# Moving the lane swaps of a spatial product on TensorE: cuts at 10, 19 and 38 of 48 instead of 12, 20 and 32

## The chip, the cores and the metric

One core of one Trainium2 chip. The metric is the device time of one execution in microseconds (us); of several runs the median is taken.

## The reference

```python
xn = _layernorm(x)                                   # x: 1 x 2048 x 512
# A: attention, 32 heads of 16
qkv = xn @ wqkv
p = softmax(q @ k.T * 16 ** -0.5); o = p @ v
A = o @ wo
# B: gated MLP with a product over the positions
z = gelu(xn @ w_in)                                  # 2048 x 1792
z1, z2 = z[..., :896], _layernorm(z[..., 896:])
g = einsum("ts,bsf->btf", w_sp, z2) + b_sp[:, None]  # w_sp: 2048 x 2048
B = (z1 * g) @ w_out
out = x + A + B
```

The step that this case is about is g, the *spatial* product: every output column block (128 of the 896 features) is a sum over all 2048 positions.

## The kernel before, in words

Everything is written out as one stream per engine by a planner that runs while the program is built. After a start of some 130 us the work goes in **rounds**. A round (the loop over `b` from L1521) holds four steps of attention: 8 score matmuls (`st`, in `score`, L1274, each followed by an exponential on ACT, `pf`, L1277), 8 matmuls for the row maxima of later scores (`mx`, in `max_one`, L904, each followed by a reduction on DVE, L905), then a share of **dense** matmuls of the other branches (one line, `lane`, L233), and at the end 16 matmuls that multiply the probabilities with v (`o`, in `pv`, L1232). So each round shows as one block of 16 `o` matmuls, and the time from one block's start to the next is the time of a round. Row maxima run 26 steps ahead of the scores. There are 256 such blocks; we number the rounds as `b` does (b = 286, 290, ...).

TensorE is used as two **lanes**: rows 0 to 63 of the array and rows 64 to 127, side by side. Scores and maxima take one lane each. A dense product has 128 rows, so it is cut into a half for each lane, and the two halves of one accumulator must not write its PSUM bank at the same time. A group of two blocks therefore has two accumulators (banks `d0`, `d1`), and `halves` (L252) gives each lane another one: a **pair** is one matmul on lane 0 for one accumulator and one on lane 1 for the other. Each accumulator has 48 products (16 tiles of 128 positions, 3 products for each tile, since numbers are split into a high and a low part), so a group has 96 pairs. `cuts` says after how many products the lanes change accumulators. With cuts (12, 20, 32) the first accumulator's products 0 to 11 go on lane 0 while the second's 0 to 11 go on lane 1; then they swap, and each lane does products 0 to 19 of the other; then 12 to 31, then 20 to 47, then 32 to 47: **runs** of 12, 20, 20, 28 and 16 pairs.

```python
for k, stop in enumerate([*cuts, total, total]):
    turn_ = k % 2
    while at[turn_] < stop:
        i, j = divmod(at[turn_], 3)
        ...
        yield END if last else SWAP if at[turn_] == stop else 1
```

A swap ends what `gather` may collect: a round holds pairs of one run only. `share` then divides the collected run evenly over rounds: a run of r pairs takes at most r // 8 rounds, and at most about 13 pairs go in one. That gives the numbers of dense pairs in a round. When a tile that a product needs isn't there by the planner's clock, the run is collected up to that product and the rest waits (`yield -2`). `fill` orders the matmuls of a round by a randomised search over its own cost model.

`spatial` (L717) has 16 groups: for each of four stripes of w_sp, three groups of two blocks and one single block of 48 pairs. For two-block groups the cuts depend on `want`, the pairs that the planner would like to place in a round: (12, 24, 36) above 11.4, (12, 20, 36) above 10.2, and the third choice below. We number the groups 0 to 15. The third choice is taken by groups 0, 1, 2, 4, 5, 6, 8, 9, 10 and 14. The z2 tiles of a group (`zs`, four quarters for each block, 512 KB each) are loaded on SP by `load_z`: a quarter is asked for in `done(s)` when both accumulators have passed tile 3, 7, 11 or 15; the first of these asks for the fourth quarter of the own group, and the planner counts it as there 0.8 + 4.0 us later at the earliest. After a group, DVE adds a row to the first accumulator (L807) and ACT copies the second (L78); both free the banks for the next group.

Of the kernel before, what the change touches and what calls it, by code (L numbers as in the profile page):

```python
# [55 lines left out]
def fused_block(ctx, tc, x, wqkv, wo, w_in, w_spT, b_sp, w_out, out):  # L56
# [19 lines left out]
    def act(out, in_, func, n, ago=1.2, **kw):  # L76
        load["A"] = max(load["A"], clock() - ago) + 0.18 + n / 1200.0
        return nc.scalar.activation(out, in_, func, **kw)  # L78

    def dve(n, rate=1):  # L80
        load["D"] = max(load["D"], clock() - 1.2) + 0.065 + n / (960.0 * rate)
        return nc.vector
# [38 lines left out]
    def move(dst, src):  # L121
        dma[0] = max(dma[0], clock()) + 0.1 + 4e-6 * math.prod(dst.shape) / FLOW
        nc.sync.dma_start(raw(dst), raw(src))
# [7 lines left out]
    def slow(us, fn, *args):  # L131
        later(us, waiting.append, (fn, args))
# [10 lines left out]
    def clock():  # L143
        return max(lanes)

    def gps(us):
        pool[0] = max(pool[0], clock()) + us
        return nc.gpsimd
# [24 lines left out]
    def later(us, fn, *args):  # L173
        late.append((clock() + us, len(late), fn, args))
# [20 lines left out]
    def piece(nm):  # L195
        return big.tile([P, 2, 512], F32R, tag="big", name=nm, bufs=RING)

    def t512(nm):
        return big.tile([P, 512], F32, tag="t512", name=nm, bufs=4)

    def hilo(nm):
        return big.tile([P, 2, 512], F32R, tag="hilo", name=nm, bufs=3)
# [22 lines left out]
    def three(lhs, rhs):  # L225


        (lh, ll), (rh, rl) = lhs, rhs
        return [(lh, rh), (ll, rh), (lh, rl)]
# [46 lines left out]
    def whole(accs, cells, done=None):  # L276


        for i in range(len(cells)):
            while True:  # L280
                prods = cells[i]()
                if prods is not None:
                    break
                yield -2
            for j in range(3):
                last = i == len(cells) - 1 and j == 2
                for half in range(2):
                    lane(accs[half], half, prods[j], i == 0 and j == 0, last)
                if j < 2:
                    yield 1  # L290
            if done:
                posts.append(partial(done, i))
            yield END if last else 1
# [8 lines left out]
    def dpair(nm):  # L302
        return [dpsum(f"{nm}_{u}", f"d{u}") for u in range(2)]
# [27 lines left out]
    def prepare(out, loads, freed=None):  # L331


        loads, flight, made = list(loads), [], []
        while loads or flight or made:
            if made and clock() >= made[0][0]:
                _, k, t = made.pop(0)
                out[k] = t
            if flight and clock() >= flight[0][0]:
                _, k, l = flight.pop(0)  # L340
                t = end(l)
                made.append((pool[0], k, t))
                rawfree.append(pool[0])
            if loads and len(rawfree) > 0 and clock() >= rawfree[0] and (freed is None or freed and clock() >= freed[0]) and (not steady or dma[0] <= clock() + BACK):
                rawfree.pop(0)
                if freed:
                    freed.pop(0)
                k, *a = loads.pop(0)
                l = begin(*a)
                flight.append((dma[0] + LAND, k, l))  # L350
            yield

    def prime():

        next(queue[1])
# [291 lines left out]
    def wait(k, gen):  # L647
        yield from until(clock() + k)
        yield from gen

    def z1_gelu(f, g, x, u):
        gelu_in(x, u, 512)
        yield from pool_done(LAG)
        yield from calm()
        act(u, u, AF.Tanh, 512, scale=GC)
        yield from ready("A")
        gelu_out(x, u, 512, 0.5)
        gelued.append((f, g))
        yield
# [53 lines left out]
    def sp_weights(g, s):  # L713
        return f"wsp{g}_{s}", w_spT[s * P:(s + 1) * P, g * 512:(g + 1) * 512], 512


    def spatial():  # L717
        zp, z1s, hls = {}, {}, {}

        def load_z(g, f, i):  # L720
            t = piece(f"zs{g}_{f}_{i}")
            move(t.rearrange("p a (s f) -> p a s f", f=P), z2scr[:, f, :, 4 * i:4 * i + 4, :])
            later(4.0, zp.update, {(g, f, i): t})

        def load_z1(g, f):
            z1s[g, f] = x = t512(f"z1i{g}_{f}")
            move(x, z1scr[f][:, g, :])
            hls[g, f] = hilo(f"hhl{g}_{f}")
            side.append(wait(10.0, z1_gelu(f, g, x, hls[g, f][:, 0, :].bitcast(F32))))

        def load_b(g):
            move(brow, b_sp[4 * g:4 * g + 4, :].rearrange("(o a) b -> o (a b)", o=1).to_broadcast([P, 512]))

        groups = [(g, [f, f + 1] if f + 1 < NF else [f]) for g in range(NG) for f in range(0, NF, 2)]
        ahead = [(g, f, i) for g, fs in groups for i in range(4) for f in fs]
        while len(stored) < NT:
            yield -1
        load_b(0)
        for _ in range(4):
            load_z(*ahead.pop(0))  # L740
        yield -4
        for _ in range(2):
            load_z(*ahead.pop(0))
        for n, (g, fs) in enumerate(groups):
            accs = dpair(f"sp{g}_{fs[0]}")
            last_, single = n == len(groups) - 1, len(fs) == 1
            if single and g + 1 < NG:
                freed = [clock()] * 2
                bg.append(prepare(wsp, [((g + 1, s), *sp_weights(g + 1, s)) for s in range(NT)], freed))

            def prods(f, s):
                zt, sl = zp[g, f, s // 4], slice((s % 4) * P, (s % 4 + 1) * P)
                w = wsp[g, s]
                return three((zt[:, 0, sl], zt[:, 1, sl]), (w[:, 0, :], w[:, 1, :]))

            def part(s):
                if (g, s) not in wsp or any((g, f, s // 4) not in zp for f in fs):
                    return None
                return prods(fs[0], s) if single else [prods(f, s) for f in fs]

            def done(s):
                if s == 7:
                    for f in fs:
                        load_z1(g, f)
                if single and g + 1 < NG:
                    freed.append(clock() + 1.0)
                if last_:
                    nonlocal_freed(s)
                if s % 4 == 3:
                    for _ in fs:  # L770
                        if ahead:
                            slow(0.8, load_z, *ahead.pop(0))

            tail = []

            def nonlocal_freed(s):
                if s == 0:
                    bg.append(prepare(wout, [(f, f"wout{f}", w_out[f * P:(f + 1) * P, :], 512) for f in range(NF)], tail))
                if s < NF:
                    tail.append(clock() + 1.0)  # L780
                if s == NT - 5:
                    prime()

            cells = [(lambda s=s: part(s)) for s in range(NT)]
            want = STEPS * pace + credit / 4
            cuts = (12, 24, 36) if want > 11.4 else (12, 20, 36) if want > 10.2 else (12, 20, 32)
            if single:
                yield from whole(accs, cells, done)
                f = fs[0]
                hl = hls[g, f]  # L790
                t = hl[:, 1, :].bitcast(F32)
                act(t, accs[0], AF.Copy, 512)
                dve(512).tensor_add(t, accs[1], t)
                gps(1.3).tensor_add(t, t, brow)
                side.append(h_split(g, f, z1s[g, f], hl))
                if g + 1 < NG:
                    later(done_by("P"), load_b, g + 1)
            else:
                yield from halves(accs, cells, cuts, done)
                for u, f in enumerate(fs):  # L800
                    hl = hls[g, f]
                    t = hl[:, 1, :].bitcast(F32)
                    if u:
                        act(t, accs[u], AF.Copy, 512)
                        gps(1.3).tensor_add(t, t, brow)  # L805
                    else:
                        dve(512).tensor_add(t, accs[u], brow)  # L807
                    side.append(h_split(g, f, z1s[g, f], hl))
            yield 0
# [815 lines left out]
```

## Time and profile before

| | us |
|---|---|
| median of 3 runs (1789.13 to 1792.41) | 1790.3 |
| the profiled execution | 1790.37 |
| its span, first to last instruction | 1788.3 |
| TensorE busy in it | 1777.3 (99%) |
| DVE busy | 1449.6 (81%) |
| ACT busy | 1267.0 (71%) |
| GpSimd (POOL) busy | 782.5 (44%) |

TensorE is busy nearly all the time, at a granted clock of 0.999, but a busy TensorE is not a TensorE at its peak: matmuls overlap, and their ends are modelled. What a round costs is read from the starts of the `o` blocks.

### The profile page before, as it was taken

To read this page: it belongs to the slowest core of one execution; us is meant where nothing else is said; L and a number is where in the kernel's file an instruction comes from. 1 tells how busy PE (TensorE), PEld (TensorE's weight loads), DVE (VectorE), ACT (ScalarE), POOL (GpSimd) and SP (SyncE) were. 2 spreads that over 40 slices of the span, in tenths; PEclk is the share of its full clock that TensorE was granted. 3 is DMA by queue.
4 is the path that set the end of the run, shared out by engine and by line. 5 is a ranking of instruction groups with operands and counts; after the bars stand their busy time and mean duration, and the time that the engine had idled before them with its cause. 6 is when DMAs were issued, how large, how long until landed. Compare 5 with 4: busy or idle time off the path is not lost.

```text
span 1788.3 us, 37962 instructions
## 1 busy us (share of the span) xinstructions
PE 1777.3 (99%) x14419; PEld 1140.7 (64%) x14419; DVE 1449.6 (81%) x2604; ACT 1267.0 (71%) x2351; POOL 782.5 (44%) x815
## 2 busy tenths in 40 slices
PE   9999999999999999999999999999999999999998
PEld 7876666666666666666666566666666666666664
DVE  5288888988888888888888888888877888888872
ACT  5338788887777777777777777777776777677765
POOL 4257676777412542257334573224765261003220
PEclk9999999999999999999999999999999999999999
DMA  7552443534645744356445564345766454454534
GB/s 282 201 171 78 133 127 104 170 88 125 198 150 172 221 140 116 109 171 183 133 144 176 173 195 115 105 126 164 200 180 179 142 169 134 149 170 150 160 108 135
DMA packets 218254, 274.63 MB, mean 154 GB/s; under 512 B 35752, under 2 KB 119352, under 8 KB 216632
## 3 DMA queue, kind: packets, MB, share of 16 engines
q1 hardware_dynamic: 215336, 263.47, 49.1%
q0 software_dynamic: 2592, 8.46, 1.2%
q8 instruction: 114, 1.87, 0.5%
q14 instruction: 68, 0.56, 0.1%
q10 hardware_dynamic: 144, 0.26, 0.0%
HBM read 178.55 MB, written 93.58 MB: 152 GB/s over the span
## 4 chain that ended last, share of the span: by engine, by line
PE 96%; DMA 1%; DVE 1%; ACT 1%; SPq 0%; issue 0%; POOL 0%; DVEq 0%; POOLq 0%; ACTq 0%
PE o L1232 26%; PE st L1274 18%; PE sp L233 17%; PE mx L904 13%; PE z2p L233 5%; PE mo L233 4%; PE z1p L233 3%; PE qk L233 3%; PE ao L233 2%; PE duo L233 2%; PE v L221 1%; PE v L222 1%; PE v L223 1%; DMA zs<-z2scr 0%; PE qk L221 0%; PE qk L222 0%
## 5 line engine op out<-in xcount | busy, mean ns | idle before, releaser
L905 DVE TENSOR_REDUCE mm<-mx 128x1 f32<-128x512 f32 x2048 | 1291.2, 685 | 249.4 <-PE mx L904 214.6
L1277 ACT ACTIVATE pf<-st 128x512 f32<-128x512 f32 x2048 | 1102.9, 601 | 361.9 <-PE mx L904 211.1
L1274 PE MATMUL st<-qst,kst 50*128 50x512 f32 x2048 | 764.4, 410 | 0.8 <-ACT pf L1277 0.7
L904 PE MATMUL mx<-kst,qst 48*128 48x512 f32 x2048 | 752.3, 412 | 0.1
L1274 PEld LDWEIGHTS st<-qst,kst 50*128 50x128 f32 x2048 | 361.0, 185 | 248.1 <-issue 116.8
L233 PE MATMUL sp<-wsp,zs 64*128 64x512 f32 x2688 | 510.2, 393 | 0.0
L1232 PE MATMUL o<-pf,vall 128*32 128x512 f32 x4096 | 492.5, 598 | 0.0
L904 PEld LDWEIGHTS mx<-kst,qst 48*128 48x128 f32 x2048 | 361.8, 185 | 63.4 <-ACT pf L1277 11.6
L233 PEld LDWEIGHTS sp<-wsp,zs 64*128 64x128 f32 x2688 | 366.2, 186 | 29.9
L1232 PEld LDWEIGHTS o<-pf,vall 128*32 128x32 f32 x4096 | 107.0, 109 | 235.2 <-issue 215.7
L233 PE MATMUL mo<-wout,hp 64*128 64x512 f32 x672 | 124.5, 392 | 0.0
L233 PEld LDWEIGHTS mo<-wout,hp 64*128 64x128 f32 x672 | 90.5, 186 | 9.6
L539 POOL TENSOR_TENSOR hhl<-z1i 128x512 f32<-128x512 f32 x28 | 29.2, 1042 | 148.0 <-DMA z1i<-z1scr 118.4
L78 ACT ACTIVATE e<-o 128x512 f32<-128x512 f32 x64 | 38.4, 599 | 70.0 <-PE o L1232 65.8
L861 POOL TENSOR_TENSOR xr<-mox,xr 128x512 f32<-128x512 f32 x8 | 10.3, 1285 | 131.3 <-ACT mox L78 131.3
L545 POOL TENSOR_SCALAR hhl<-hhl 128x512 f32<-128x512 f32 x28 | 17.4, 621 | 104.0 <-ACT hhl L78 104.0
L967 POOL TENSOR_TENSOR ob<-ob 128x512 f32<-128x512 f32 (+1 forms) x16 | 20.7, 1292 | 96.3 <-DMA ob<-rscr 96.3
L805 POOL TENSOR_TENSOR hhl<-hhl,brow 128x512 f32<-128x512 f32 x12 | 15.4, 1287 | 83.5 <-ACT hhl L78 80.7
L233 PE MATMUL ao<-wo,op 64*128 64x512 f32 x288 | 51.9, 392 | 0.0
L586 POOL TENSOR_TENSOR z<-z,z2u 128x896 fp32r<-128x896 f32 x16 | 34.1, 2130 | 27.4 <-ACT z2u L78 27.4
L1039 POOL TENSOR_TENSOR fin<-aox,fin 128x512 f32<-128x512 f32 x8 | 10.3, 1282 | 74.9 <-ACT aox L78 74.9
L233 PEld LDWEIGHTS ao<-wo,op 64*128 64x128 f32 x288 | 36.4, 186 | 4.1
(293 smaller groups left out, 1955.6 us busy)
## 6 DMA issues: line engine op xcount, KB each, us to landing
zs<-z2scr SPq DMA_DIRECT2D x112, 512.0 KB
escr<-e SPq DMA_DIRECT2D x60, 256.0 KB
hscr<-hhl SPq DMA_DIRECT2D x28, 512.0 KB
xscr<-xnT POOLq DMA_DIRECT2D x16, 512.0 KB, 4.9
qscr<-qkhl SPq DMA_DIRECT2D x16, 512.0 KB
kscr<-qkhl SPq DMA_DIRECT2D x16, 512.0 KB
qst<-qscr SPq DMA_DIRECT2D x128, 64.0 KB
hp<-hscr SPq DMA_DIRECT2D x16, 512.0 KB
```

The source lines that it names most:

```text
L78: return nc.scalar.activation(out, in_, func, **kw)
L221: nc.tensor.matmul(acc, lh, rh, start=first, stop=False)
L222: nc.tensor.matmul(acc, ll, rh, start=False, stop=False)
L233: made[half] = lambda: nc.tensor.matmul(acc, prod[0][rows], prod[1][rows], start=start, stop=stop)
L539: gps(0.0022 * n).tensor_mul(u, x, x)
L586: gps(2.1).tensor_sub(low, z, u)
L904: nc.tensor.matmul(acc, qst[c][rows, t * P:(t + 1) * P], kst[p % 2][rows, kc * 512:(kc + 1) * 512], start=True, stop=True)
L905: nc.vector.tensor_reduce(mmax[i // 16][:, j, t, kc:kc + 1], acc, AX.X, ALU.max)
L967: gps(1.3).tensor_mul(both[rows, 0, :], both[rows, 0, :], both[rows, 2, :])
L1232: nc.tensor.matmul(acc[cols:cols + VW, a:a + w], vpack(kt - 1 + r, 2 * p + j), pf[:, j * 512 + a:j * 512 + a + w], start=kt == 1 and a == ...
L1274: nc.tensor.matmul(st, kst[p % 2][rows, kt * P:(kt + 1) * P], qst[c][rows, :], start=True, stop=True)
L1277: nc.scalar.activation(full[n][:, j * 512:(j + 1) * 512], st, AF.Exp, scale=0.25)
```

## The change

The third choice of `cuts` becomes (10, 19, 38): runs of 10, 19, 28, 29 and 10 pairs, 96 as before, with four swaps as before.

```diff
-            cuts = (12, 24, 36) if want > 11.4 else (12, 20, 36) if want > 10.2 else (12, 20, 32)
+            cuts = (12, 24, 36) if want > 11.4 else (12, 20, 36) if want > 10.2 else (10, 19, 38)
```

Counted in the order of the built programs, the dense pairs in the rounds of a group are:

| groups | before | changed |
|---|---|---|
| 1, 2, 4, 5, 6, 8, 9 | 12, 10 10, 10 10, 10 9 9, 8 8 | 10, 10 9, 9 9 10, 10 10 9, 10 |
| 0 | the same | 10, 10 9, 12 14 2, 10 10 9, 10 |
| 10 | the same | 10, 10 9, 13 13 2, 10 10 9, 10 |
| 12 to 14 (27 rounds, b = 710 to 814) | 12 times 12; 11 11 13 13; five 10; three 9; two 8; one 3 | 19 times 12; 15 11 10; three 9; 6; 3 |
| the rounds after that | the same numbers | the same, one round earlier |
| last round of all (b = 1022) | 12 | 0 |

Before, the cuts of group 12 and 13 were (12, 24, 36) and group 14 had the third choice; in the changed program all three have (12, 24, 36), since by its counts `want` is higher when they begin. Groups 0 to 11 begin at the same steps in both programs.

Three places show what moves on TensorE (PE). The names: `st` is a score, `mx` a row maximum, `sp` a spatial product with its accumulator's number, `wsp` and `zs` its operands, `o` the product with v. First, the beginning of the round b = 470, the first of group 5, before:

```order
L1274 MATMUL st_0_12953<-qst_86,kst_90 128x512
L904 MATMUL mx_1_12961<-kst_90,qst_88 128x512
L1274 MATMUL st_0_12964<-qst_86,kst_90 128x512
L1274 MATMUL st_1_12973<-qst_86,kst_90 128x512
L904 MATMUL mx_0_12976<-kst_90,qst_88 128x512
L233 MATMUL sp_2_1_12952<-wsp_0_11512,zs_3_0_12593 128x512
L233 MATMUL sp_2_0_12951<-wsp_0_11512,zs_2_0_12574 128x512
```

and in the changed program:

```order
L1274 MATMUL st_1_12951<-qst_86,kst_90 128x512
L904 MATMUL mx_0_12961<-kst_90,qst_88 128x512
L233 MATMUL sp_2_1_12950<-wsp_0_11523,zs_3_0_12667 128x512
L233 MATMUL sp_2_0_12949<-wsp_0_11523,zs_2_0_12657 128x512
L904 MATMUL mx_1_12966<-kst_90,qst_88 128x512
L1274 MATMUL st_0_12969<-qst_86,kst_90 128x512
```

The first dense matmul stood sixth and now stands third, ahead of three matmuls of attention. Second, the round b = 674 of group 10 in the changed program, whole but for its `o` block (before, the same round has 20 dense matmuls):

```order
L1274 MATMUL st_0_17603<-qst_87,kst_89 128x512
L904 MATMUL mx_1_17607<-kst_89,qst_88 128x512
L233 MATMUL sp_4_1_17151<-wsp_12_15491,zs_5_3_17480 128x512
...
L233 MATMUL sp_4_0_17150<-wsp_12_15491,zs_4_3_17465 128x512
L1274 MATMUL st_1_17644<-qst_87,kst_89 128x512
L233 MATMUL sp_4_1_17151<-wsp_12_15491,zs_5_3_17480 128x512
L233 MATMUL sp_4_0_17150<-wsp_12_15491,zs_4_3_17465 128x512
L904 MATMUL mx_0_17649<-kst_89,qst_88 128x512
```

These four dense matmuls (two pairs) are all that was left of the run: the two that read the fourth quarter `zs_4_3`, `zs_5_3`. Third, the end of the last round, b = 1022, in the changed program:

```order
L1274 MATMUL st_1_25859<-qst_88,kst_90 128x512
L1274 MATMUL st_0_25863<-qst_88,kst_90 128x512
L1274 MATMUL st_1_25866<-qst_88,kst_90 128x512
L1274 MATMUL st_0_25870<-qst_88,kst_90 128x512
L1232 MATMUL o_3_25694<-pf_25811,vall 32x512 x2
L1232 MATMUL o_3_25694<-pf_25818,vall 32x512 x2
L1232 MATMUL o_3_25694<-pf_25861,vall 32x512 x2
L1232 MATMUL o_3_25694<-pf_25868,vall 32x512 x2
```

Before, 24 dense matmuls stand between the third of these scores and the fourth; they have moved to earlier rounds.

## Rows read from the trace of the kernel before

**Rows 1.** The page: span, busy time of each engine, costliest DVE group.

```profile
span 1788.3 us, 37962 instructions
...
PE 1777.3 (99%) x14419; PEld 1140.7 (64%) x14419; DVE 1449.6 (81%) x2604; ACT 1267.0 (71%) x2351; POOL 782.5 (44%) x815
...
L905 DVE TENSOR_REDUCE mm<-mx 128x1 f32<-128x512 f32 x2048 | 1291.2, 685 | 249.4 <-PE mx L904 214.6
```

**Rows 2.** Timeline (start us, us, instruction), PE, group 5: its `o` blocks.

```profile
886.49 1.92 PE L1232 MATMUL o<-pf,vall 128*32 128x512 f32 x16
...
893.22 1.92 PE L1232 MATMUL o<-pf,vall 128*32 128x512 f32 x16
...
899.48 1.92 PE L1232 MATMUL o<-pf,vall 128*32 128x512 f32 x16
...
905.73 1.92 PE L1232 MATMUL o<-pf,vall 128*32 128x512 f32 x16
...
912.12 1.92 PE L1232 MATMUL o<-pf,vall 128*32 128x512 f32 x16
...
918.37 1.92 PE L1232 MATMUL o<-pf,vall 128*32 128x512 f32 x16
...
924.67 1.92 PE L1232 MATMUL o<-pf,vall 128*32 128x512 f32 x16
...
930.76 1.92 PE L1232 MATMUL o<-pf,vall 128*32 128x512 f32 x16
...
937.03 1.93 PE L1232 MATMUL o<-pf,vall 128*32 128x512 f32 x16
...
943.14 1.92 PE L1232 MATMUL o<-pf,vall 128*32 128x512 f32 x16
...
949.14 1.92 PE L1232 MATMUL o<-pf,vall 128*32 128x512 f32 x16
```

**Rows 3.** Timeline, PE: `o` blocks around a round of 13 and of 3 pairs.

```profile
1276.51 1.92 PE L1232 MATMUL o<-pf,vall 128*32 128x512 f32 x16
...
1283.45 1.06 PE L1232 MATMUL o<-pf,vall 128*32 128x512 f32 x8
```

```profile
1309.70 1.92 PE L1232 MATMUL o<-pf,vall 128*32 128x512 f32 x16
...
1315.78 1.92 PE L1232 MATMUL o<-pf,vall 128*32 128x512 f32 x16
```

**Rows 4.** Timeline, b = 406 (first round of single group 3, 8 pairs).

```profile
787.15 1.92 PE L1232 MATMUL o<-pf,vall 128*32 128x512 f32 x16
...
788.47 0.68 DVE L807 TENSOR_TENSOR hhl<-sp,brow 128x512 f32<-128x512 f32 x1
...
789.01 0.50 PE L1274 MATMUL st<-qst,kst 50*128 50x512 f32 x1
789.07 0.18 DVE L918 TENSOR_REDUCE mrow<-mm 128x8 fp32r<-128x32 f32 x1
...
789.20 0.50 PE L233 MATMUL sp<-wsp,zs 64*128 64x512 f32 x1
...
789.67 0.21 DVE L924 STREAM_TRANSPOSE ms<-mrow 128x32 f32<-128x32 f32 x1
```

```profile
793.79 1.49 PE L1232 MATMUL o<-pf,vall 128*32 128x512 f32 x12
```

**Rows 5.** Timeline, PE and ACT, the last round, b = 1022.

```profile
1771.00 1.92 PE L1232 MATMUL o<-pf,vall 128*32 128x512 f32 x16
...
1776.29 1.92 PE L1232 MATMUL o<-pf,vall 128*32 128x512 f32 x16
```

```profile
1769.59 2.12 ACT L1277 ACTIVATE pf<-st 128x512 f32<-128x512 f32 x4
1773.39 1.58 ACT L1277 ACTIVATE pf<-st 128x512 f32<-128x512 f32 x3 [1.68 <-PE st L1274]
1776.41 0.60 ACT L1277 ACTIVATE pf<-st 128x512 f32<-128x512 f32 x1 [1.45 <-PE st L1274]
```

**Rows 6.** Timeline, SP, group 5: the fourth-quarter loads.

```profile
901.46 0.94 SPq L123 DMA_DIRECT2D zs<-z2scr  x2
```

## The prediction

> **What bounds the kernel now.** I read the page first: PE is busy 99% of the span, DVE 81%, and DVE's largest group, 2048 reductions over the row maxima, takes 1291.2 us, 0.63 us each [rows 1]. A busy share of 99% doesn't say that PE's own work sets the pace, so I went on to the timeline and took the starts of the `o` blocks through one group whose runs are known, 12, 20, 20, 28 and 16 pairs, cut into rounds of 12, 10, 10, 10, 10, 10, 9, 9, 8, 8. Their lengths are 6.73, 6.26, 6.25, 6.39, 6.25, 6.30, 6.09, 6.27, 6.11 and 6.00 us, together 62.65 [rows 2]. The reader is to see two things in them. First, a pair is not worth the same everywhere: from 10 pairs to 12 a pair costs some 0.22 us, from 9 to 10 about 0.18, from 8 to 9 about 0.04. Below 9 there is a floor: a round with only 3 pairs still takes 6.08 us, while one of 13 takes 6.94 [rows 3]. Second, every fourth round is 0.12 to 0.18 longer (6.39 among tens, 6.27 among nines), whatever its share; those places are the same in both programs, so they drop out.
>
> Below the floor something other than PE's stream sets the round. DVE is the nearest: eight reductions are 8 x 0.63 = 5.0 us [rows 1], and with latencies between scores, exponentials and free PSUM banks that comes to about 6.
>
> So the change is a redistribution. No matmul, copy or load is added or removed: 96 pairs and four swaps for each group before and after. What it can win or lose is the bend in that curve, and the waits at the places where the order is new.
>
> **The change part by part.** Prices: 12 pairs 6.73, 10 pairs 6.27, 9 pairs 6.09, 8 pairs 6.11 and 6.00 [rows 2]; 13 pairs 6.94, 3 pairs 6.08 [rows 3]. The rounds that no row shows are estimates from these. 14 and 15 pairs: 6.94 plus 0.24 for each further pair, 7.18 and 7.42; their bounds are 6.94 (nothing more) and twice that step. 2 and 6 pairs: 6.08 and 6.05, between the rows of 3 and of 8; from below they can't be under DVE's 5.0. 11 pairs, halfway: 6.49.
>
> *Seven regular groups* (1, 2, 4, 5, 6, 8, 9). Rounds of 12, 8 and 8 become 10, 9 and 9, the others keep their number: 6.73 + 6.11 + 6.00 = 18.84 against 6.27 + 6.09 + 6.09 = 18.45, a gain of 0.39. If the 6.11 belongs to the place (the round before a group's last) and a round of 8 is worth 6.00, it is 0.28. I take 0.3, times 7: **-2.1 us**.
>
> *Group 0 and group 10.* The third run reaches product 38, and products from 36 read the fourth quarter of z2, which isn't asked for before both accumulators have passed product 12. Before that was pair 24 of the group; now it is pair 31, two pairs into that same run. The planner therefore collects the run without its last two pairs. In seven groups it spreads what it has over rounds so that the two rejoin (9 9 10); in these two groups it spends the 26 pairs in two rounds and leaves a round of 2. Group 0: 8 + 8 become 14 + 2, 12.11 against 7.18 + 6.08 = 13.26, +1.15. Group 10: 12 + 8 + 8 become 13 + 13 + 2, 18.84 against 13.88 + 6.08 = 19.96, +1.12. Together **+2.3 us**.
>
> *Groups 12 to 14.* They follow other cuts, but the planner's book-keeping has changed, and 12 pairs more are placed in these 27 rounds. Struck out what both have, 11, two 13, four 10 and two 8 stand against seven 12, a 15 and a 6: 6.49 + 13.88 + 25.08 + 12.11 = 57.56 against 47.11 + 7.42 + 6.05 = 60.58: **+3.0 us**. After that both programs run the same sequence one round apart, at no difference.
>
> *The last round* has lost the 12 pairs. Before, it held its last score back behind them, and that exponential started at 1776.41; the last `o` block, begun at 1776.29, lasted 1.92, to 1778.21, 1.20 after that exponential's end [rows 5]. Without the pairs four exponentials can follow each other from 1773.39, in 2.12 as four do just before [rows 5], to 1775.5; 1.20 later is 1776.7: **-1.5 us**. The tail after it is unchanged.
>
> *The first round of each new group* is short now, 10 pairs, and its first dense matmul stands third instead of sixth. It needs the banks that the group before leaves: DVE's L807 and ACT's copy. The nearest place in the trace is the first round of single group 3, where a dense matmul stands second: L807 ends at 789.15 and the dense matmul starts at 789.20; the five small instructions that end a chunk of row maxima follow it, from 789.07 by the row's start to 789.88; and the round lasts 6.64 where 8 pairs take 6.00 [rows 2, 4]. DVE's work in such a round is 0.68 + 0.81 + 8 x 0.63 = 6.5 us; 12 pairs (6.73) covered it, 10 pairs (6.27) don't. That falls together in three of the nine groups (1, 5, 9). The cost of one lies between nothing (DVE's backlog is let into the next round, which has 1.2 us of room for it) and the 0.64 of that row; I take 0.3, near DVE's excess: **+0.9 us**. In the other six DVE has 5.7 us of work and 6.27 of room: nothing, with 0.64 each as the far end.
>
> *Loads.* SP's queue has the same loads. The fourth quarter was issued at 901.46, in the third round of its group [rows 2, 6]; now it comes some 7 pairs, 4 to 5 us, later, near 906, and is needed near the end of the sixth round, about 923. The cover is some 17 us; I put nothing down. The later release of `zs` buffers moves what SP waits for by the same 4 us, in groups of 62 us.
>
> Sum: -2.1 + 2.3 + 3.0 - 1.5 + 0.9 = **+2.6 us**. On the profiled execution's 1790.37 that is 1793.0; the median of the runs is 1790.3, the same within 0.1. What a measurement of this kernel can tell from no change is about 0.2%, 3.6 us, so I forecast a change too small to tell, on the slow side.
>
> **The rivals.**
>
> *Every new first round stalls.* Mechanism: the dense matmul in third place waits for the eviction, and since PE starts matmuls in order, the scores and maxima behind it come late, then ACT and DVE. For it: b = 406 loses 0.64 with the dense matmul in second place [rows 4]. Against it: in second place it starts 0.19 after the score, and there L807 has just ended; in third place both lanes have a matmul of attention ahead of it, which gives it the 0.2 us of a pair more. If all nine pay 0.64, the sum has 5.8 in place of 0.9: +7.5, 1797.9, slower. It decides from the point where L807 ends more than some 0.4 us after the round's first score. That a matmul can't overtake another is also what the Trainium skill says ("TensorE: Matmul & The Clock Gate", Part 2: What happens when you issue a matmul); the rows of b = 406 agree with it. Chance 0.20.
>
> *A pair is worth the same everywhere.* If PE alone set the rounds, at 0.22 us a pair, evening out would win nothing, the rounds of 2 would cost nothing, and only the 12 pairs moved from the last round count: 12 x 0.22 - 1.5 = +1.1, 1791.5, no measurable change. The rows from 10 to 13 pairs speak for it, the row of 3 pairs (6.08) against [rows 2, 3]. The Trainium skill has the rule (the same page, section "Wait — 56ns, not 53.3ns?"): back-to-back matmuls of 512 columns start about 216 ns apart at the full clock; the steps between 10 and 13 agree with it, the step from 8 to 9 doesn't. Chance 0.15.
>
> *The late quarter.* If the z2 quarter lands after its use, PE stands for the rest; with, say, 2 us in each of nine groups, 18 more, 1811. No wait of PE for `zs` stands in the list of waits. Chance 0.03.
>
> *Faster.* The regular groups win 0.39 each, and the rounds of 2 and 6 pairs shrink towards DVE's 5.0 us instead of the 6.08 seen with 3: -2.7 + 0.1 + 2.0 - 1.5 = -2.1; with the 0.64 at the first rounds of the single groups 3 and 7 gone as well (the round ahead of them has 10 pairs, not 8, so DVE's backlog is smaller) -3.4, 1787.0, and a little more makes it measurable. Chance 0.05.
>
> **How the numbers follow.** The forecast has 0.57. Its own spread, from first rounds at nothing and regular groups at 0.39 (2.6 - 0.9 - 0.6 = +1.1) to first rounds at 0.64 in three groups and the rounds of 14 and 15 at twice the step (2.6 + 1.0 + 0.7 = +4.3), puts 0.40 within 0.2% and 0.17 above. Same: 0.40 + 0.15 = 0.55. Slower: 0.17 + 0.20 + 0.03 = 0.40. Faster: 0.05. The time is the forecast's, 1793.0. The range goes from 1789.0 (below the equal-price rival, and the scatter of the runs) to 1798.0 (all first rounds stall).
>
> **What would show it.** In the changed profile the `o` blocks of group 5 should span 62.3 us instead of 62.65; the first rounds of groups 1, 5 and 9 should take 6.5 to 6.6, those of groups 2, 4, 6 and 8 about 6.27; group 0 and 10 should each be longer than before by 1.1, with a round near 6.1 for the two pairs; the last `o` block should follow its forerunner sooner and end 5.7 us after that one's start instead of 7.2. First rounds of 6.9 everywhere would mean the stall; a round of 2 pairs near 5 us would mean that the floor isn't one; a wait of PE for `zs` would mean that the load was cut too fine. I am wrong if the regular groups don't get shorter at all, or if the 27 rounds of groups 12 to 14 cost nothing more.

## The result and the profile after

| | before | after |
|---|---|---|
| median, 20 runs each, side by side | 1790.9 us (1789.13 to 1792.46) | 1794.24 us (1793.03 to 1797.95) |
| ratio, 95% interval | | 1.0021 [1.0015, 1.0028] |
| span of the profiled execution | 1788.3 | 1792.5 |
| granted clock in it | 0.999 | 0.999 |

The change costs 3.3 us, 0.21%. The interval leaves out 1, so 20 runs of each do tell it from nothing, where the prediction took 0.2% for the least that can be told. The forecast was +2.6 (1793.0), too small to tell and on the slow side: the direction is right and the size is near. But the sum came about in another way than it was worked out: what the terms priced came to less, and 2.7 us (in the profiled execution) come from two waits that no term had.

The page of the changed kernel shows no difference in busy time, as it must with the same work (rows 1 answer to it):

```profile
span 1792.5 us, 37989 instructions
...
PE 1778.0 (99%) x14419; PEld 1139.5 (64%) x14419; DVE 1450.0 (81%) x2604; ACT 1267.0 (71%) x2351; POOL 781.0 (44%) x815
...
L905 DVE TENSOR_REDUCE mm<-mx 128x1 f32<-128x512 f32 x2048 | 1291.8, 684 | 254.6 <-PE mx L904 221.1
```

So the reading goes by rounds, from one `o` block to the next. The timeline of PE in group 5 (start us, us, instruction), where [rows 2] had 62.65 us:

```profile
887.91 1.92 PE L1232 MATMUL o<-pf,vall 128*32 128x512 f32 x16
...
894.27 1.92 PE L1232 MATMUL o<-pf,vall 128*32 128x512 f32 x16
...
900.56 1.93 PE L1232 MATMUL o<-pf,vall 128*32 128x512 f32 x16
...
906.65 1.92 PE L1232 MATMUL o<-pf,vall 128*32 128x512 f32 x16
...
912.92 1.92 PE L1232 MATMUL o<-pf,vall 128*32 128x512 f32 x16
...
944.00 1.92 PE L1232 MATMUL o<-pf,vall 128*32 128x512 f32 x16
...
950.26 1.93 PE L1232 MATMUL o<-pf,vall 128*32 128x512 f32 x16
```

The group takes 62.35, 0.30 less, as forecast for it. Its first round has 10 pairs and takes 6.36, not the 6.5 to 6.6 that were expected of it. The same view of group 0 has the rounds of 12, 14 and 2 pairs:

```profile
618.97 1.93 PE L1232 MATMUL o<-pf,vall 128*32 128x512 f32 x16
...
625.68 1.92 PE L1232 MATMUL o<-pf,vall 128*32 128x512 f32 x16
...
632.83 1.93 PE L1232 MATMUL o<-pf,vall 128*32 128x512 f32 x16
...
638.91 1.93 PE L1232 MATMUL o<-pf,vall 128*32 128x512 f32 x16
```

They are 6.71, 7.15 and 6.08 us. Group 10 has 6.95 and 6.93 for its two rounds of 13 and 6.07 for its round of 2. The end of the program, PE and then ACT, which answers to [rows 5]:

```profile
1776.84 1.92 PE L1232 MATMUL o<-pf,vall 128*32 128x512 f32 x16
...
1779.36 3.04 PE L1232 MATMUL o<-pf,vall 128*32 128x512 f32 x16
```

```profile
1779.23 2.06 ACT L1277 ACTIVATE pf<-st 128x512 f32<-128x512 f32 x4 [1.20 <-PE st L1274]
```

The last block ends at 1782.40, 5.56 us after its forerunner's start (7.21 before, 5.7 forecast). It starts early and stretches to 3.04; ACT's four exponentials end at 1781.29, 1.11 us before it does, as 1.20 before.

The whole span by stretches, each from the start of one `o` block to that of another (us, both profiled executions; the last column is what the prediction's terms gave):

| stretch | before | after | difference | forecast |
|---|---|---|---|---|
| before group 0 (the same instructions in both programs, so one execution against another) | 599.00 | 600.22 | +1.22 | 0 |
| group 0 | 62.98 | 63.71 | +0.73 | +1.15 |
| groups 1 to 9, without singles | 438.37 | 437.84 | -0.53 | -2.1 + 0.9 |
| singles 3 and 7 | 73.50 | 72.59 | -0.91 | 0 |
| group 10 | 62.61 | 63.70 | +1.09 | +1.12 |
| single 11 | 26.83 | 26.79 | -0.04 | 0 |
| groups 12 to 14 (b = 710 to 814) | 175.74 | 179.66 | +3.92 | +3.0 |
| b = 818 to 958 | 231.64 | 232.32 | +0.68 | 0 |
| b = 962 to 1018 | 100.33 | 100.02 | -0.31 | 0 |
| last round and tail | 17.29 | 15.63 | -1.66 | -1.5 |

The +1.22 ahead of group 0 is scatter: in other runs with these same instructions there the stretch takes 598.2 to 601.2.

Two rounds stand out against their shares. The one of b = 750, 12 pairs, lasts 8.33 us instead of 6.71, and that of b = 926, 12 pairs too, 7.82. Neither place has such a round in the kernel before. PE in the first of them:

```profile
1328.91 1.92 PE L1232 MATMUL o<-pf,vall 128*32 128x512 f32 x16
...
1332.76 0.47 PE L1274 MATMUL st<-qst,kst 50*128 50x512 f32 x1 [1.26 <-DVE mm L905]
...
1337.24 1.92 PE L1232 MATMUL o<-pf,vall 128*32 128x512 f32 x16
```

The release is put down to a DVE reduction, but that one had long been done: the score reads a new chunk, whose row maxima come back into `qst` by way of DRAM. DVE's transpose makes the tile `ms`, SP stores it (`mscr<-ms`), and a second transfer reads it (`qst<-mscr`). In the run of the first experiment below, which has the same wait, the profile names that transfer:

```profile
1333.06 0.47 PE L1274 MATMUL st<-qst,kst 50*128 50x512 f32 x1 [1.37 <-DMA qst<-mscr]
```

DVE, POOL and SP in that stretch of the changed kernel:

```profile
1318.45 0.21 DVE L924 STREAM_TRANSPOSE ms<-mrow 128x32 f32<-128x32 f32 x1
```

```profile
1317.47 0.62 POOL L545 TENSOR_SCALAR hhl<-hhl 128x512 f32<-128x512 f32 x1 [5.89 <-ACT hhl L78]
...
1321.38 1.28 POOL L967 TENSOR_TENSOR ob<-ob 128x512 f32<-128x512 f32 x1
...
1323.41 1.30 POOL L972 TENSOR_TENSOR ohl<-ob,ohl 128x512 fp32r<-128x512 f32 x1
```

```profile
1315.40 1.25 SPq L123 DMA_DIRECT2D os<-escr  x2
1324.74 1.59 SPq L123 DMA_DIRECT2D ob<-escr  x2
1326.42 0.40 SPq L123 DMA_DIRECT2D mscr<-ms  x1
1330.62 1.33 SPq L123 DMA_DIRECT2D qst<-mscr  x2
```

The store was ready at 1318.66 and was issued at 1326.42, 7.8 us later. Ahead of it in SP's queue stands `ob<-escr`, a load for the normalisation of attention (`norm_out`), which needs the only `ob` buffer. Its last reader, POOL's L972, ended at 1324.71. SP's list of waits names POOL's instruction right behind that one:

```profile
SPq L123 <- POOL os L958: 8.3, 1, 8.3
```

In the kernel before, the same load is ahead of the same store, but POOL had done L967 to L972 before its two L545 and L546, not after them:

```profile
1314.50 1.28 POOL L972 TENSOR_TENSOR ohl<-ob,ohl 128x512 fp32r<-128x512 f32 x1
...
1317.09 0.62 POOL L545 TENSOR_SCALAR hhl<-hhl 128x512 f32<-128x512 f32 x1 [1.30 <-ACT hhl L78]
```

```profile
1315.81 1.20 SPq L123 DMA_DIRECT2D ob<-escr  x2
...
1317.98 0.35 SPq L123 DMA_DIRECT2D mscr<-ms  x1
...
1322.04 1.33 SPq L123 DMA_DIRECT2D qst<-mscr  x2
```

At b = 926 it is the same store of another chunk, and here the profile names the transfer at once:

```profile
1617.85 1.92 PE L1232 MATMUL o<-pf,vall 128*32 128x512 f32 x16
...
1621.18 0.47 PE L1274 MATMUL st<-qst,kst 50*128 50x512 f32 x1 [0.74 <-DMA qst<-mscr]
...
1625.66 1.92 PE L1232 MATMUL o<-pf,vall 128*32 128x512 f32 x16
```

```profile
1611.48 1.64 SPq L123 DMA_DIRECT2D os<-escr  x2
...
1614.63 0.46 SPq L123 DMA_DIRECT2D mscr<-ms  x1
...
1618.97 1.37 SPq L123 DMA_DIRECT2D qst<-mscr  x2
```

The transpose ended at 1607.68, and `mscr<-ms` was issued at 1614.63, 7.0 us later. It isn't POOL this time: `os<-escr`, which SP had ahead of it, waited 3.2 us for the transfer `escr<-e` to land. In the kernel before, the store stands ahead of those loads:

```profile
1602.53 0.34 SPq L123 DMA_DIRECT2D mscr<-ms  x1
...
1608.08 1.54 SPq L123 DMA_DIRECT2D os<-escr  x2
```

### The profile page after: what moved, and what is told of

Read it like the earlier page. It is cut to its first block, busy times and chain, and to the rows that moved or that the text cites. A ratio compares the mean times of both kernels' runs of the same rounds, so it can differ in the third digit from the quotient of the medians.

```text
span 1792.5 us, 37989 instructions
## 1 busy us (share of the span) xinstructions
PE 1778.0 (99%) x14419; PEld 1139.5 (64%) x14419; DVE 1450.0 (81%) x2604; ACT 1267.0 (71%) x2351; POOL 781.0 (44%) x815
## 4 chain that ended last, share of the span: by engine, by line
PE 95%; DMA 2%; DVE 1%; ACT 1%; SPq 0%; issue 0%; POOL 0%; DVEq 0%; ACTq 0%; POOLq 0%
PE o L1232 26%; PE st L1274 18%; PE sp L233 17%; PE mx L904 12%; PE z2p L233 5%; PE mo L233 4%; PE z1p L233 3%; PE qk L233 2%; PE ao L233 2%; PE duo L233 2%; DMA z1scr<-z 0%; DMA wsp_3r<-in_w_spT 0%; PE v L221 0%; PE v L222 0%; PE v L223 0%; DVE mm L905 0%
## 5 line engine op out<-in xcount | busy, mean ns | idle before, releaser
L967 POOL TENSOR_TENSOR ob<-ob 128x512 f32<-128x512 f32 (+1 forms) x16 | 20.6, 1290 | 92.8 <-DMA ob<-rscr 81.4
L545 POOL TENSOR_SCALAR hhl<-hhl 128x512 f32<-128x512 f32 x28 | 17.3, 619 | 69.8 <-ACT hhl L78 69.8
```

The lines of the kernel that those rows point to most:

```text
L545: gps(0.0011 * n).tensor_scalar(u, u, a, a, ALU.mult, ALU.add)
L967: gps(1.3).tensor_mul(both[rows, 0, :], both[rows, 0, :], both[rows, 2, :])
```

## The experiments

Theory: the round curve read from the trace prices all that the change moves; two waits in SP's queue, 1.62 + 1.11 us, come on top. Rivals: the short first rounds of the new groups stall; the late store isn't what the scores wait for.

**The new cuts in groups 0 and 10 alone.**

```diff
-            cuts = (12, 24, 36) if want > 11.4 else (12, 20, 36) if want > 10.2 else (10, 19, 38)
+            cuts = (12, 24, 36) if want > 11.4 else (12, 20, 36) if want > 10.2 else (10, 19, 38) if n in (0, 10) else (12, 20, 32)
```

> New cuts in groups 0 and 10 alone, the old ones in all others. By its counts group 0 is uneven as in the changed kernel (12, 14, 2), group 10 comes out regular (9 9 10), the single groups 3 and 7 follow a round of 8 as before, and from b = 710 on the TensorE order is the changed kernel's, row for row. Theory (the bend of the round curve prices the change, and two late row-maximum transfers come on top): against before group 0 +0.7, group 10 -0.2, groups 12 to 14 +2.3, last round -1.7, together +1.1 us; and if the waits at b = 750 and b = 926 belong to the order from b = 710 on, they come back with 1.6 and 1.1, together +3.8 us (1794.7). Rival (the cost sits in the short first rounds of the regular groups): those are gone, so no more than +0.5 us.

Measured: 1793.63 us, ratio 1.0019 [1.0010, 1.0027], so the new cuts in two of the ten groups bring as much loss as those in all ten, within the intervals. Group 0 takes 63.66, groups 12 to 14 take 179.94, and both waits come again (8.44 and 7.96). The rival falls: there is no new first round in the seven regular groups here. Group 10 takes only 62.35: shifted by the rest of the order, the planner had the fourth quarter in time there and made rounds as in a regular group, with none of 2 pairs. So the +1.09 of group 10 isn't in this run, and a stall in one round (7.20 at b = 510, where a score waits 0.23 us for `qst<-mscr`) makes up for part of it.

**The new cuts everywhere but in groups 0 and 10.**

```diff
-            cuts = (12, 24, 36) if want > 11.4 else (12, 20, 36) if want > 10.2 else (10, 19, 38)
+            cuts = (12, 24, 36) if want > 11.4 else (12, 20, 36) if want > 10.2 else (12, 20, 32) if n in (0, 10) else (10, 19, 38)
```

> Old cuts in groups 0 and 10, new ones in the seven regular groups (group 14 gets the middle choice by itself). By its counts groups 12 to 14 have 12 pairs more than before here too, in four rounds of 12 in place of 10, 10, 8 and 8. Theory: regular groups -0.5 us, single groups 3 and 7 -0.9, groups 12 to 14 +2.2, last round -1.7, together -0.9 us (1790.0) unless a late transfer holds a score again; groups 0 and 10 exactly as before (63.0 and 62.6 us). Rival (the cost sits in the regular groups): slower than before by 2 us or more.

Measured: 1790.45, ratio 1.0001 [0.9992, 1.0010]. No wait at b = 750 or 926 (6.72, 6.73). Groups 12 to 14 still take 2.0 us more than before, the last round is short, and groups 1 to 9 with their singles take 1.35 less.

**All stores of row maxima on ACT's queue**, to take them out from behind SP's loads. PE's order is the same.

```diff
-        move(mscr[g % 4].rearrange("b k x -> (b k) x"), ms)
+        dma[0] = max(dma[0], clock()) + 0.1 + 4e-6 * math.prod(ms.shape) / FLOW; nc.scalar.dma_start(raw(mscr[g % 4].rearrange("b k x -> (b k) x")), raw(ms))
```

> The changed kernel; the store of the row maxima (mscr from ms, 64 of them) is issued by ACT's queue instead of SP's; every TensorE instruction stands where it stood. Theory: the waits at b = 750 (8.33 us) and b = 926 (7.82) come from that store standing in SP's queue behind another load that waits; both rounds go back to 6.7, -2.7 us, about 1791.5. Rival (the maxima themselves are late because the rounds ahead are short): both rounds stay above 7.5 and the time stays at 1794.2.

Measured: 1799.88, ratio 1.0058 [1.0044, 1.0072], not the 1791.5 of the theory. The two rounds did come back to 6.70 and 6.71, but b = 278 now takes 14.98 us. ACT's timeline there:

```profile
593.36 0.33 ACTq L932 DMA_DIRECT2D mscr<-ms  x1
593.79 1.57 ACT L1277 ACTIVATE pf<-st 128x512 f32<-128x512 f32 x3 [6.38 <-DMA z1scr<-z]
```

The transpose that fills `ms` had ended at 586.38, so the store waited for something else, by the profile for another transfer to land, and the exponentials stood behind it. On SP the same store goes out late as well (10.0 us after its transpose in the changed kernel), without an engine behind it that computes. **The same edit on the kernel before** was the control:

> The kernel before with the same move of the row maximum store to ACT's queue, a control. Before has no round with such a wait, so theory: no change within 1 us of 1790.9. If the move by itself is worth 2 us here, then the gain of the changed kernel with it says nothing about the two waits.

Measured: 1801.81, ratio 1.0062 [1.0049, 1.0074], with the same stall at b = 278 (15.45), against an expectation of no change. So the edit costs 11 us of its own, and the pair of runs settled nothing on the total: with it the changed kernel is even 1.9 us the faster, since the control has further stalls at b = 510, 518 and 726 (0.7 to 0.9 us each) that the other lacks. It needed a smaller edit.

**Only the two stores that were late**, of 64, on ACT's queue:

```diff
-        move(mscr[g % 4].rearrange("b k x -> (b k) x"), ms)
+        dma[0] = max(dma[0], clock()) + 0.1 + 4e-6 * math.prod(ms.shape) / FLOW; (nc.scalar if g in (47, 58) else nc.sync).dma_start(raw(mscr[g % 4].rearrange("b k x -> (b k) x")), raw(ms))
```

> The changed kernel with only two of the 64 stores of row maxima (those of the chunks whose first scores, at b = 750 and b = 926, waited 1.6 and 1.1 us) issued by ACT instead of SP; PE's order is the same. Theory (head of line in SP's queue): both rounds come back to 6.7 us, nothing else moves, span some 2.7 us shorter, median about 1791.5. Rival (the row is late for another reason, or ACT loses what SP wins, as in the run with all 64 stores): the rounds stay at 8.3 and 7.8 or another round near them grows by as much, median 1794.

Measured: 1791.63, ratio 1.0010 [1.0001, 1.0019]. That is 1.4 us above the kernel before in the same set of runs, where the changed kernel was 3.3 above in its own: 2.0 us won (2.6 if the two medians are taken as they are). ACT, SP and PE around b = 750:

```profile
1322.72 0.35 ACTq L932 DMA_DIRECT2D mscr<-ms  x1
```

```profile
1327.81 1.43 SPq L123 DMA_DIRECT2D ob<-escr  x2
1329.34 1.30 SPq L123 DMA_DIRECT2D qst<-mscr  x2
```

```profile
1331.97 1.92 PE L1232 MATMUL o<-pf,vall 128*32 128x512 f32 x16
...
1338.66 1.92 PE L1232 MATMUL o<-pf,vall 128*32 128x512 f32 x16
```

The load `ob<-escr` is as late as it was (POOL is), but the store no longer stands behind it and goes out 1.0 us after its transpose instead of 7.8. So `qst<-mscr` goes out 2.6 us before the round's `o` block instead of 1.7 after, and the round takes 6.69. b = 926 takes 6.71. **The same two stores on the kernel before:**

> The same edit on the kernel before, where no score waits at these places: a control. Theory: no change, 1790.4 plus or minus 0.7. If the edit costs something by itself (ACT held up by a store that waits), it shows here, with a round near b = 742 or 918 longer than in the kernel before.

Measured: 1790.48, ratio 1.0001 [0.9992, 1.0010], and no round near b = 742 or 918 grew. So the two waits come from the late stores, and cost 1.64 and 1.11 us in their rounds: this is shown. The medians, 2.0 to 2.6 us, agree, but with intervals of some 1.2 and 1.6 us either way they wouldn't prove it alone. The Trainium skill ("DMA: Bandwidth & Descriptors", section "Issuing engines are not separate DMA queues") says that starting transfers from several engines saves only the issuing time, usually small. This case measures otherwise: issuing a 16 KB store took 0.4 us, but another queue let it go out 6.8 us earlier, since the entry ahead of it on SP waited 8.3 us.

**The new cuts in the seven regular groups, and nothing else** (groups 0, 10 and 14 keep the old ones):

```diff
-            cuts = (12, 24, 36) if want > 11.4 else (12, 20, 36) if want > 10.2 else (10, 19, 38)
+            cuts = (12, 20, 32) if n == 14 else (12, 24, 36) if want > 11.4 else (12, 20, 36) if want > 10.2 else (12, 20, 32) if n in (0, 10) else (10, 19, 38)
```

> The new cuts in the seven regular groups alone; groups 0, 10 and 14 keep 12, 20 and 32, so groups 12 to 14, the long part behind them and the last round are as before. Theory (curve of a round's length): regular groups 0.1 to 0.2 us shorter each, single groups 3 and 7 0.4 each, first rounds nothing more: 1.4 to 1.8 us less than before, 1789.0. Against the run with group 14 also changed (1790.45) it tells what groups 12 to 14 (+2.0) and the last round (-1.7) come to. Rival (the first rounds' stalls eat the gain): 1790.4 or more.

Measured: 1789.35, ratio 0.9996 [0.9987, 1.0005], 0.9 less where 1.4 to 1.8 were expected. Groups 1 to 9 with their singles take 510.70 against 511.87 before, -1.2 us; the median's 0.9 can't be told from nothing by itself. The profiled execution has a late store too: at b = 798 the round takes 7.04 instead of 6.27, a score waits for `qst<-mscr`, and `mscr<-ms` was issued 8.1 us after its transpose. The rounds there have the pairs that they have in the kernel before, so such a wait doesn't need the new order of groups 12 to 14.

**The third cut at 36 instead of 38**, where a run needs nothing of the fourth quarter of z2:

```diff
-            cuts = (12, 24, 36) if want > 11.4 else (12, 20, 36) if want > 10.2 else (10, 19, 38)
+            cuts = (12, 24, 36) if want > 11.4 else (12, 20, 36) if want > 10.2 else (10, 19, 36)
```

> The same change with a third cut at 36 instead of 38, so that no run has to go without the fourth quarter of z2: no round of 2 pairs behind a 13 or 14 is forced by it, the order shifts in all groups, and the last round keeps its 12 pairs. By the curve of a round's length the rounds sum to 1.8 us less than before (1168.1 against 1169.9 over the groups): 1788.6. Theory: 1788 to 1791 as long as SP's queue makes no new score wait; each such wait adds 1 to 2 us. Rival (the bend of the curve isn't what the change turned on): 1793 to 1795, as with 38.

Measured: 1787.87, ratio 0.9987 [0.9979, 0.9996], 2.4 us faster than the kernel before. No round of 2, 3 or 6 pairs is in it, and no round around b = 750 or 926 lasts longer than its share. The rival falls. The gain isn't in the regular groups, which take what they took: group 0 carries 10 pairs more for 1.54 us (64.52) and groups 12 to 14 another 10 for 0.43 (176.17), and in return single 11 (25.18) and b = 818 to 958 (229.54) carry 18 fewer and give back 1.65 and 2.10. So the cut moved work all through the program, and that its place at the data's boundary is what helped isn't shown by itself.

## Why the prediction was right, and where it wasn't

**The curve: right to hundredths.** Each size that no row showed came out at its estimate: 14 pairs 7.15 (7.18), 15 pairs 7.41 (7.42), 2 pairs 6.08 (6.08), 6 pairs 6.04 (6.05), 11 pairs 6.48 (6.49). A round of 2 costs what a round of 8 costs, so the rival in which a pair is worth the same everywhere is out. The floor goes with DVE, as the prediction supposed. In the rounds of 8 pairs of single 3 in the changed kernel, which last 5.99, DVE does eight reductions back to back in 5.06 us and waits 0.93 us for the first `mx` behind the `o` block, together 5.99:

```profile
803.64 5.06 DVE L905 TENSOR_REDUCE mm<-mx 128x1 f32<-128x512 f32 x8 [0.93 <-PE mx L904]
```

That is a reading of rows; no run changes DVE's work to test it.

**Groups 0 and 10: right.** Measured +0.73 and +1.09 for +1.15 and +1.12. Group 0 would be nearer, had the first round of the kernel before not lasted 7.16 in that execution; in the control with two stores on ACT, which has the same order as before, the group took 62.53, and against that the new 63.71 is +1.18.

**Groups 12 to 14: the term was too large by some 0.5 us, and a wait came on top.** The +3.92 are 1.62 of the wait and 2.30. With the store moved, the stretch took 178.19, +2.45 against before, for +3.0. The ten-pair rounds that fell away had been priced too low, as two of them took 6.42 and 6.38 (b = 782, 786) and not 6.27, and the rounds of 12 that replaced them too high, at 6.73 for 6.71.

**Regular groups and first rounds: both terms were too large, and their sum was met by luck.** Groups 1 to 9 with their singles gave back 1.44, 1.35, 1.41, 1.21 and 1.17 us in the five profiles that have the new cuts there, for a forecast of -2.1 + 0.9 = -1.2. But the singles, for which nothing was put down, have 0.91 of the changed kernel's 1.44; the seven groups alone gave back 0.53. The first term was over-sized: a round of 8 is worth 6.00 and the 6.11 belonged to its place, which the text had as the second possibility, so it is -0.25 a group, -1.75. The first rounds cost less than feared at groups 1, 5 and 9 (6.34, 6.36 and 6.33 against 6.27, some 0.07 each instead of 0.3), but not nothing elsewhere: all seven together have 0.7 more than 6.27 each, the largest behind the single groups (6.55 and 6.44). Small stalls of 0.2 to 0.3 in three other rounds (b = 402, 526, 630) took as much; what those wait for is open.

**Singles 3 and 7: missed.** They won 0.35 and 0.56, and the prediction put nothing down; it had them only within a rival of small chance, with the reason that the round ahead has 10 pairs and not 8. The runs bear that out: their first rounds take 6.28 to 6.32 and 6.22 to 6.24 in all five kernels that have 10 pairs ahead, and 6.63 to 6.78 in the four that have 8; in the kernel with the third cut at 36, which has 12 ahead, both take 6.08 (b = 402 and 546 there). The rows of b = 406 after, beside [rows 4]:

```profile
788.93 1.93 PE L1232 MATMUL o<-pf,vall 128*32 128x512 f32 x16
...
790.12 0.68 DVE L807 TENSOR_TENSOR hhl<-sp,brow 128x512 f32<-128x512 f32 x1
790.72 0.17 DVE L918 TENSOR_REDUCE mrow<-mm 128x8 fp32r<-128x32 f32 x1
...
790.86 0.50 PE L233 MATMUL sp<-wsp,zs 64*128 64x512 f32 x1
```

From the `o` block L807 starts after 1.19 us instead of 1.32, and the dense matmul after 1.93 instead of 2.05. That is the direction that DVE's smaller backlog would give, but only 0.12 of the 0.34 that the round won, so the rest of the reason is argued and not shown.

**The last round: right**, -1.66 for -1.5.

**Loads: the step that failed.** "I put nothing down" held for what it looked at, the fourth quarter's cover. The load was later than worked out, 22.2 us after the start of group 5 (15.0 before), 7.2 us later instead of 4 to 5, and still no score or dense matmul waited for it:

```profile
910.13 0.41 SPq L123 DMA_DIRECT2D zs<-z2scr  x1
...
911.09 0.43 SPq L123 DMA_DIRECT2D zs<-z2scr  x1
```

But the step stopped at z2's own transfers. It asked what a later load does to its reader and not what the new order does to the other entries of SP's queue. "After that both programs run the same sequence one round apart, at no difference" is the sentence that was wrong for b = 926, and the term of groups 12 to 14, where b = 750 lies, priced pairs alone. PE's sequence is the same, POOL's and SP's relative to it is not, and at two of 64 chunks a store with no slack came to stand behind a load that waited, at b = 750 for a buffer that POOL hadn't freed yet, at b = 926 for another transfer to land. That cost 2.7 us. The rival with a wait in it was the wrong wait: no first round reached 6.9.

In sum: without the two waits the change costs 1791.63 - 1790.26 = 1.4 us, at the edge of what 11 runs tell from nothing, and the stretches from group 0 on, in the two profiled executions, come to 0.2 without them. The forecast of +2.6 was near +3.3 because waits that it didn't have made up for terms that were too high and for the singles' gain that it missed. The directions and the curve were understood; that the number came so near is in part luck.

## What to carry to other kernels

A table of a stage's length against its share of work, read from the trace, prices a redistribution, where nothing stalls, to a few hundredths of a us for each stage, and shows where a smaller share no longer pays: here below 8 pairs a round gives nothing back. Then go through each in-order queue that the new order shifts against the others, and for each entry with a waiting reader ask what stands ahead of it and what that one waits for, a buffer or a landing. A cut that makes a run read past data that isn't there yet is worth trying at the data's boundary (36 here was the fastest, though it moved much else); and moving an entry to another queue should be done for the few that are late, since the queue of an engine that computes holds that engine up too.

## What the runs showed of the hardware that was not expected

A store issued by ACT holds ACT: 6.38 us without an exponential, and 8 us of the round at b = 278, for one 16 KB transfer whose data were ready but which by the profile waited for another to land. That ACT's queue is strictly first in, first out is also in the Trainium skill ("PSUM — Partial Sum Buffer", section "Engine vs sequencer instructions"); the rows above agree.

The granted clock fell once behind a thin round. In the profiled execution of the kernel with two stores on ACT, the round of 2 pairs in group 0 is followed by an `o` block of 3.62 us instead of 1.92. The table by windows of 4 us (us, PE busy, PEld, DVE, ACT, POOL with their counts, granted clock, DMA share, GB/s):

```profile
636.00:640.00 4.00, 3.95 (x24) 2.10 (x24) 3.73 (x7) 4.00 (x8) 0.00 (x0) 1.00 0.29 98
640.00:644.00 4.00, 4.00 (x20) 1.04 (x22) 1.98 (x8) 0.61 (x2) 0.00 (x0) 0.58 0.06 15
644.00:648.00 4.00, 4.00 (x38) 3.29 (x38) 3.90 (x7) 3.65 (x7) 1.85 (x3) 1.00 0.81 241
```

The clock was at 0.58 of full speed over the second of these 4 us stretches, so for most of it at the lower of the two levels, 1.2 GHz; in the 4 us before, 24 matmuls are counted, and 38 in those after. The round cost 8.00 us instead of 6.26, and this was also the slowest of that kernel's 11 executions, at 1795.31. The changed kernel's own profile has the same 24 matmuls there and a full clock, so a thin round doesn't always bring it on, and that it was the cause isn't shown. In the changed kernel's own 20 runs the six slowest, 1795.51 to 1797.95, are those with a mean clock of 0.998 or 0.997; where in them the clock fell no profile shows.
